# Reordered first loads and a re-timed plan in a fused polysketch attention and ReGLU kernel

## The chip, the cores and the metric

The kernel runs on one core of a Trainium2 chip. The metric is device time in microseconds of one execution, the median over runs. A core has five engines with a queue each: TensorE (PE in the profile, its weight loads PEld), VectorE (DVE), ScalarE (ACT), GpSimd (POOL) and SyncE (SP), which only issues DMAs here. ScalarE can issue DMAs too. Each engine works through its own queue in order and waits on semaphores where data is not there yet. All DMAs run on the same 16 DMA engines.

## The reference

```python
# q, k, v: [4 batches, 4 heads, 1088, 32]; S1, S2: [8, 32]
def phi(x):
    a = einsum('rd,bhsd->bhsr', S1, x)
    b = einsum('rd,bhsd->bhsr', S2, x)
    return einsum('bhsi,bhsj->bhsij', a, b).reshape(..., 64)
q_p, k_p = phi(q), phi(k)
kv  = einsum('bhsf,bhsd->bhfd', k_p, v)
z   = k_p.sum(over s)
num = einsum('bhsf,bhfd->bhsd', q_p, kv)
den = einsum('bhsf,bhf->bhs', q_p, z) + 1e-6
x   = (num / den), heads side by side: [4352 tokens, 128]
out = (relu(x @ w_gate) * (x @ w_val)) @ w_out     # d_ff = 1536
```

Linear attention with a feature map of degree two, then a gated feed-forward layer (FFN) on its output, all in float32 at the borders and mostly in fp16 inside.

## The kernel before

**The stages.** For each batch b the K side (class `K`) loads k, transposes it on VectorE in 32x32 blocks (`kt1`, tile `kT`), sketches it on TensorE (`ksk`), transposes back (`kt2`, tile `kab`), forms the products of the feature map (`kphi`, tile `kp`) on POOL and, for batch 0 in part, on VectorE, casts v to fp16 on ScalarE (`vc`, L599) and multiplies (`kv`, L606). The result is scaled and masked into `bz` on VectorE (`kve`, L613). The Q side (class `Q`, and `G` for a group of 256 or 512 tokens) does likewise with q; the products are `qqp` (L859). They are transposed by TensorE for the first three groups and by a DMA transpose for the other seven (`TURN`; `xpose`, L867), multiplied with `bz` (`num`, L893) and written as x, tile `xT`. The first group is divided by its denominator on VectorE (`x_div`, L900), the others earlier.

**The FFN** (class `F`) is cut into units of at most 512 columns. A unit is: `g` (x with a block of w_gate, L950), relu out of PSUM on ScalarE (L955), `v` (x with w_val, L962), the product on VectorE (L972), and `o` (with w_out, L984). Every sixth unit takes another way: ScalarE copies the `v` result out of PSUM (L967) and POOL multiplies (L977). There are ten groups: 256, 256, 512, then six of 512 and a last of 256 tokens. The weights come as float32 in thirds (`wg0`, `wv0`, `wo0`, ...), into buffers that later hold k, q and v of other batches, and are cast to fp16 by ScalarE or POOL (`CAST`, L425 and L427).

**What sets the order.** The kernel is scheduled by hand: a planner (class `Plan`) gets every step with its engine, an assumed duration (`busy`, `rec`), what it comes after, the PSUM banks that it takes, and a due time. It also gets assumed landing times of the first loads (`LAND`, L404). It plays the steps through, and then they are issued in the order of their planned starts. The planned times do nothing else: on the chip each engine goes through its queue in this order, and waits are for data, buffers and banks alone. `T0` and `U` give a due time to each FFN unit (`T0 + u * U`), from which the others' are worked back.

**The first loads** do not go through the planner. They are issued on SP at the top of the program in this order: k of batch 0 in two pieces, q of batch 0 in two, v of batch 0 in four quarters of 32 partitions (`load_v`, 144 KB each), then the weights' thirds with k of batch 1 among them, and q of batch 1 (L231 to L270). The loads of the later batches are planned steps on SP (`load`, L435), each behind the casts that free its buffer. A DMA takes one of eight semaphores in turn, in order of issue over both issuing engines, and is issued once the DMA that had that semaphore before it has landed.

**Dummies.** `warm(n)` (L326) issues matmuls of a zero tile into a spare PSUM bank, some n columns in all, in pieces of up to 128 columns. The plan's gaps on TensorE before the first FFN matmul are filled with them.

Of the kernel before, what the change touches and what calls it, by code (L numbers as in the profile page):

```python
# [146 lines left out]
def kernel(  # L147
# [87 lines left out]
    nc.sync.dma_start(out=q_sb[0][:, QA:], in_=flat(q, 0)[:, QA:])  # L235
    for a in (0, 2, 1, 3):
        load_v(nc.sync, 0, a)
# [24 lines left out]

    load_w(0)
    load_w(1)
    load_wo(0)
    load_k(nc.sync, 1)
    load_w(2)
    load_wo(1)
    load_wo(2)
    nc.sync.dma_start(out=q_sb[1], in_=flat(q, 1))  # L270

# [54 lines left out]
    def warm(n):  # L326

        while n >= 32:
            m = min(n // 32 * 32, 128)
            nc.tensor.matmul(PS[:, W_BANK, 0:m], zero, zero[:, 0:m], start=True, stop=True)  # L330
            n -= m

# [46 lines left out]
    PE0, WARM = 4.15, 8.0  # L379
    P = Plan({"PE": PE0, "DVE": 3.3, "ACT": 4.2, "POOL": 3.8, "SP": 13.3, "DMA": 0.0}, range(7))  # L380
    P.banks[W_BANK] = 13.0
    P.banks[S_BANK] = 6.0
    l_sx = Lease()
    T0, U, SLACK = 11.0, 0.68, 0.25
    D1 = 0.2
# [12 lines left out]
    def act(cols):  # L398
        return cols / 1200.0 + 0.045

    def pool(cols):
        return cols * 0.00188 + 0.07

    LAND = {"k0a": 3.6, "S": 4.3, "k0b": 4.25, "q0a": 5.6, "q0b": 7.35, "v0": 9.95,  # L404
            "wg0": 10.35, "wv0": 11.0, "wg1": 11.65, "wv1": 12.3, "wo0": 12.95, "k1": 15.6,
            "wg2": 16.25, "wv2": 16.9, "wo1": 17.5, "wo2": 18.1, "q1": 19.5}
    land = {n: P.landed(n, t) for n, t in LAND.items()}
    P.free["DMA"] = LAND["q1"]

    def bank(l, i=0):  # L410
        return PS[:, l.banks[i]]

    ws_op = P.add("ACT", "wS", 0.36, make_wS, [land["S"]], rec=0.13)
    wq_op = P.add("POOL", "wq", 0.25, make_wq, [ws_op])
    sa_op = P.add("DVE", "SA", 0.22, make_SA, [land["S"]], rec=0.07)
    wb_op = P.add("DVE", "WB", 0.15, make_WB, [land["S"]], rec=0.07)

    CAST = {"wg0": "ACT", "wv0": "POOL", "wg1": "ACT", "wv1": "POOL", "wo0": "POOL",
            "wg2": "ACT", "wv2": "ACT", "wo1": "ACT", "wo2": "POOL"}
    wcast = {}  # L420
# [12 lines left out]


    def load(name, fn, after):  # L435
        n = 4 if name[0] == "v" else 1
        i = P.add("SP", f"{name} issue", 0.44 * n, fn, after, rec=1.95 - 0.44 * n)
        land[name] = P.add("DMA", name, 2.7 if n == 4 else 1.4, None, [i], rec=0.15)

    load("v1", lambda: load_vs(1), [wcast["wo2"]])  # L440
    load("k2", lambda: load_k(nc.sync, 2), [wcast["wo0"], wcast["wo1"]])
    load("q2", lambda: load_q(nc.sync, 2), [])
    load("v2", lambda: load_vs(2), [wcast["wg2"], wcast["wv2"], land["v1"]])
    load("k3", lambda: load_k(nc.sync, 3), [wcast["wg0"], wcast["wv0"], land["q2"]])
    load("q3", lambda: load_q(nc.sync, 3), [wcast["wg1"], wcast["wv1"], land["q2"]])
    load("v3", lambda: load_vs(3), [land["v2"]])

    class K:


        def __init__(self, b, prev):
# [14 lines left out]
            for n, l in enumerate(self.las):  # L466
                self.sks.append(P.add(
                    "PE", f"ksk {b} {n}", sk32(KX * 32) + 0.04 if b else (0.62, 0.68)[n],
                    lambda n=n: self.sk(n), t1 + [ws_op], take=[l]))
# [17 lines left out]
            cut = [(0, 2), (2, 4), (4, 6), (6, KX)] if b else [(0, 2), (2, 4), (4, 6), (6, 8), (8, KX)]  # L487
            own = [3, 4] if b == 0 else []
            lb = Lease()
# [141 lines left out]
    class Q:  # L631
# [3 lines left out]
        def __init__(self, b, x0, n, i, ks, qt1, old):  # L635
# [9 lines left out]
            if first:  # L645
                la, lc = Lease(), Lease()
                self.la, self.lc = la, lc
                s1 = [P.add("PE", f"qsk {name} {x}", 0.48, lambda x=x: self.sk_tok(x, x + 2),
                            qt1 + [wb_op], take=[la]) for x in range(0, n, 2)]
                t2 = P.add("ACT", f"qt2 {name}", act(2 * cols), self.t2_tok, s1 + old, drop=[la],  # L650
                           rec=0.13)
                la.left += n
                lt = Lease()
                self.lt = lt
                at = P.add("PE", f"qaT {name}", 0.85, self.aT, qt1 + [sa_op], take=[lt])
                ate = P.add("ACT", f"qaTe {name}", act(256), self.aTe, [at], drop=[lt], rec=0.13)
                s2 = [P.add("PE", f"qc {name}", 0.45, self.cx, [ate, ks[0].zc_op], take=[lc])]
                o1 = P.add("DVE", f"bw {name}", dve(cols) + 0.03, self.mul_ps, s2 + [t2] + old,
                           drop=[lc], rec=0.09)
                e, eng = "DVE", nc.vector  # L660

            else:
                self.l4 = [Lease(2), Lease(2)]
                s1 = P.add("PE", f"qsk {name}", cols / 600.0 + 0.28 + 0.37 * (n > NX),
                           self.sk, qt1 + wcs + [wq_op], take=self.l4)
# [133 lines left out]
    class G:  # L799


        def __init__(self, qs, b, ks, x0, n, i, col, old, how):
# [12 lines left out]
            else:  # L815
                phis.append(P.add("POOL", f"qphi {name}", pool(n * 256),
                                  lambda: self.phi(nc.gpsimd, 0, n), [qs.o4] + old))
            if how == "DMA":
                pt = P.add("SP", f"qtd {name}", 1.28, self.xpose, phis + old, rec=0.7)
                pt = P.add("DMA", f"qtd {name}", 0.6, None, [pt], rec=0.5)  # L820
            else:
# [85 lines left out]
    class F:  # L907


        def __init__(self, u, grp, qg, js, prev, old):  # L910
# [13 lines left out]
                      due=t + 0.35)  # L924
            vv = P.add("PE", f"v {u}", cost, self.v, [qg.x_op, wcast[f"wv{third}"]], take=[lv], due=t + 0.2)
# [117 lines left out]
    for n, (b, x0, w, parts) in enumerate(sets):  # L1043
# [6 lines left out]
        for gb, y, m in parts:  # L1050
# [80 lines left out]
```

## Time and profile before

| what | value |
|---|---|
| median of 3 runs | 101.46 us (101.31 to 104.93) |
| profiled execution | 102.56 us, of which the span of instructions is 100.8 |
| granted TensorE clock | 1.000 |
| PE / PEld busy | 95.1 / 66.4 us |
| DVE / ACT / POOL busy | 83.8 / 82.2 / 59.9 us |
| moved by DMA | 13.28 MB, mean 132 GB/s |
| PE's part in the chain that ended last | 78% |

The span runs from the first instruction to the last; the execution's own time has 1.8 us around it. Busy time of TensorE is the time in which a matmul is under way, and matmuls are pipelined, so a busy TensorE can still be losing time between them. The chain that ended last is followed back from the last instruction, at each step to what released it.

```profile
L330 PE MATMUL ps<-zero 128*128 128x128 f16 (+2 forms) x85 | 7.7, 257 | 1.0 <-DVE maskkv L295 1.0
L593 POOL TENSOR_TENSOR kp<-kab 128x512 f16<-128x512 f32 (+1 forms) x15 | 17.1, 1162 | 5.0 <-DVE kab L549 5.0
L859 POOL TENSOR_TENSOR qqp<-qan,qabc 128x1024 f16<-128x1024 f32 (+1 forms) x9 | 15.7, 1763 | 0.1
```

Three rows of the costliest groups: line, engine, operation, output and inputs with their shapes, count; then busy us, mean ns of one; then the idle time of the engine just before them and what ended it.

### The profile page before, as it was taken

How to read it: one execution, taken by the hardware profiler on the slowest of the kernel's cores; microseconds unless marked ns; L12 is line 12 of the kernel's file. 1: busy time of each engine (PE TensorE's matmuls, PEld its weight loads, DVE VectorE, ACT ScalarE, POOL GpSimd, SP SyncE). 2: the span in 40 equal slices, each digit the busy share in tenths (PEclk: the TensorE clock that was granted, in tenths of full speed). 3: DMA queues.
4: the chain of work that ended last, by engine and by line, in shares of the span. 5: the costliest groups of instructions: out<-in, count | busy, mean ns of one | idle time of the engine just before them, and what ended most of it. 6: DMA issues, size and time to landing. Idle time of an engine off the chain costs nothing.

```text
span 100.8 us, 3139 instructions
## 1 busy us (share of the span) xinstructions
PE 95.1 (94%) x1191; PEld 66.4 (66%) x1191; DVE 83.8 (83%) x181; ACT 82.2 (82%) x162; POOL 59.9 (59%) x64
## 2 busy tenths in 40 slices
PE   6999997999999899999999999999999999999960
PEld 6959895678775466656756676667666666667940
DVE  5989959899999989999998679978768587795960
ACT  3411968997999978999977769899899999989940
POOL 7157269399999399349973993489960314033100
PEclk9999999999999999999999999999999999999999
DMA  2999999499943696300426003001481300120031
GB/s 44 321 272 294 408 403 417 166 309 272 386 131 108 145 136 163 104 7 0 104 52 156 7 0 104 7 7 37 121 182 37 81 24 0 52 59 0 4 100 52
DMA packets 16783, 13.28 MB, mean 132 GB/s; under 512 B 8064, under 2 KB 14464, under 8 KB 16768
## 3 DMA queue, kind: packets, MB, share of 16 engines
q1 hardware_dynamic: 16736, 13.08, 45.8%
q8 instruction: 9, 0.15, 0.6%
q14 instruction: 6, 0.05, 0.1%
q10 hardware_dynamic: 32, 0.00, 0.0%
HBM read 9.14 MB, written 2.23 MB: 113 GB/s over the span
## 4 chain that ended last, share of the span: by engine, by line
PE 78%; POOL 7%; ACT 5%; DMA 3%; issue 2%; DVE 2%; ACTq 0%
PE ps L984 19%; PE ps L950 18%; PE ps L962 17%; PE ps L330 7%; POOL qqp L859 4%; PE ps L893 3%; ACT g_sb L955 3%; PE ps L728 3%; DMA qpt<-qqp 3%; PE ps L536 2%; PE ps L606 2%; POOL kp L593 1%; PE ps L564 1%; PE ps L877 1%; DVE qabc L734 1%
## 5 line engine op out<-in xcount | busy, mean ns | idle before, releaser
L972 DVE TENSOR_TENSOR ht<-g_sb,ps 128x512 f16<-128x512 f16 (+1 forms) x87 | 55.4, 672 | 10.1 <-ACT g_sb L955 5.5
L955 ACT ACTIVATE g_sb<-ps 128x512 f16<-128x512 f32 (+1 forms) x103 | 57.1, 610 | 4.9 <-PE ps L950 4.1
L950 PE MATMUL ps<-xT,wg 128*128 128x512 f16 (+1 forms) x120 | 38.3, 348 | 0.4 <-ACT wg L425 0.4
L984 PEld LDWEIGHTS <-ht 128*128 128x128 f16 x408 | 28.8, 98 | 14.0 <-POOL ht L977 2.5
L984 PE MATMUL ps<-wo,ht 128*128 128x128 f16 x408 | 36.5, 219 | 0.2
L962 PE MATMUL ps<-xT,wv 128*128 128x512 f16 (+1 forms) x120 | 36.5, 348 | 0.0
L977 POOL TENSOR_TENSOR ht<-g_sb,v_sb 128x512 f16<-128x512 f16 x16 | 18.7, 1170 | 19.3 <-ACT v_sb L967 13.2
L593 POOL TENSOR_TENSOR kp<-kab 128x512 f16<-128x512 f32 (+1 forms) x15 | 17.1, 1162 | 5.0 <-DVE kab L549 5.0
L962 PEld LDWEIGHTS <-wv 128*128 128x128 f16 x120 | 13.0, 115 | 5.1 <-issue 1.1
L859 POOL TENSOR_TENSOR qqp<-qan,qabc 128x1024 f16<-128x1024 f32 (+1 forms) x9 | 15.7, 1763 | 0.1
L950 PEld LDWEIGHTS <-wg 128*128 128x128 f16 x120 | 13.1, 114 | 3.7 <-issue 0.9
L967 ACT COPY v_sb<-ps 128x512 f32<-128x512 f32 x16 | 9.7, 605 | 0.0
L330 PE MATMUL ps<-zero 128*128 128x128 f16 (+2 forms) x85 | 7.7, 257 | 1.0 <-DVE maskkv L295 1.0
L330 PEld LDWEIGHTS <-zero 128*128 128x128 f16 x85 | 6.7, 119 | 1.4 <-DVE maskkv L295 1.0
L992 ACT ACTIVATE o_sb<-ps 128x512 f32<-128x512 f32 (+1 forms) x10 | 5.5, 546 | 1.9 <-PE ps L984 1.9
L599 ACT CAST v<-v 128x576 f16<-128x576 f32 x8 | 5.3, 700 | 1.5 <-DMA v<-in_v_dram 1.4
L734 DVE STREAM_TRANSPOSE qabc<-ps 128x512 f32<-128x512 f32 (+2 forms) x8 | 5.4, 695 | 0.7 <-PE ps L728 0.6
L1024 DVE STREAM_TRANSPOSE qT<-q_sb 128x576 f32<-128x576 f32 (+4 forms) x10 | 6.0, 611 | 0.0
L905 ACT CAST xT<-ps 128x512 f16<-128x512 f32 (+1 forms) x9 | 4.9, 550 | 1.1 <-PE ps L893 1.1
L893 PE MATMUL ps<-qpt,bz 128*128 128x512 f16 (+2 forms) x26 | 5.3, 305 | 0.4 <-DMA qpt<-qqp 0.4
L525 DVE STREAM_TRANSPOSE kT<-k_sb 128x544 f32<-128x544 f32 (+2 forms) x8 | 5.6, 725 | 0.0
L606 PEld LDWEIGHTS <-kp 128*128 128x128 f16 (+1 forms) x72 | 3.6, 98 | 1.3 <-issue 0.2
(85 smaller groups left out, 63.9 us busy)
## 6 DMA issues: line engine op xcount, KB each, us to landing
v<-in_v_dram SPq DMA_DIRECT2D x15, 144.0 KB, 4.5
out_dram<-o_sb SPq DMA_DIRECT2D x28, 64.0 KB, 1.7
k_sb<-in_k_dram SPq DMA_DIRECT2D x3, 544.0 KB, 5.4
q_sb<-in_q_dram SPq DMA_DIRECT2D x3, 544.0 KB, 7.1
k_sb<-in_moe_w_out_dram SPq DMA_DIRECT2D x2, 256.0 KB, 5.9
q_sb<-in_q_dram SPq DMA_DIRECT2D x1, 416.0 KB, 5.2
k_sb<-in_k_dram SPq DMA_DIRECT2D x1, 288.0 KB, 2.9
k_sb<-in_k_dram SPq DMA_DIRECT2D x1, 256.0 KB, 3.0
```

Source lines behind the costliest of these rows:

```text
L330: nc.tensor.matmul(PS[:, W_BANK, 0:m], zero, zero[:, 0:m], start=True, stop=True)
L593: eng.tensor_tensor(out=self.kp[:, lo:hi].rearrange("p x g (i a c) -> p (x g i) a c", i=2, a=R), in0=src[:, 0, :, :, None].to_broadcast([1 ...
L734: nc.vector.transpose(self.abc[:, 0:self.n, 2 * i:2 * i + 2].rearrange("p x h f -> p h x f"), PS[:, b0:b1 + 1, 0:self.n * 32].rearrange("p ...
L859: eng.tensor_tensor(out=self.qp[:, lo:hi].rearrange("p x g (i a c) -> p (x g i) a c", i=2, a=R), in0=a_in[:, :, :, None].to_broadcast([128 ...
L893: nc.tensor.matmul(o[:, 0:n * 128].rearrange("f (x t) -> f x t", x=n)[:, :, t], self.ks[b or 0].bz[:, p], self.pt[:, 0:n, p, t], start=(p ...
L950: nc.tensor.matmul(bank(self.lg)[:, y * W:(y + 1) * W], wblock(wg, j), x, start=True, stop=True, skip_group_check=True)
L955: nc.scalar.activation(out=self.gs[:, 0:self.cols], in_=bank(self.lg)[:, 0:self.cols], func=ACTF.Relu)
L962: nc.tensor.matmul(bank(self.lv)[:, y * W:(y + 1) * W], wblock(wv, j), x, start=True, stop=True, skip_group_check=True)
L967: nc.scalar.copy(out=self.vs, in_=bank(self.lv))
L972: nc.vector.tensor_tensor(out=self.ht[:, 0:w], in0=self.gs[:, 0:w], in1=bank(self.lv)[:, 0:w], op=ALU.mult)
L977: nc.gpsimd.tensor_tensor(out=self.ht, in0=self.gs, in1=self.vs, op=ALU.mult)
L984: nc.tensor.matmul(o[:, s], self.ht[:, y * W + s * 128:y * W + (s + 1) * 128], wo[:, j // 4, (j % 4) * DM:(j % 4 + 1) * DM], start=(j == 0 ...
```

## The change

- v of batch 0: quarters 0 and 1 stay on SP, quarters 2 and 3 are issued by ScalarE, behind its step `wS`.
- The weights, k of batch 1 and q of batch 1 become a planned step on SP (`ring`) that the planner sets behind ScalarE's issue. Their order among themselves is as before.
- `warm` makes dummies of up to four times 128 columns in one matmul; from 8.0 us of planned time on, 0.1 us of each gap is left unfilled.
- The casts of `wv2` and `wo1` go from ScalarE to POOL.
- For batch 0, VectorE keeps only the last kp block (`own = [4]`); the fourth goes to POOL.
- The loads of k, q and v of batch 3 are put behind the DMA transpose of the fifth group (`gs[4].turn`); those of k and q no longer wait for q of batch 2.
- `LAND`, `U` and durations of several steps are changed.

```diff
-    for a in (0, 2, 1, 3):
+    for a in (0, 1):
         load_v(nc.sync, 0, a)
...
         while n >= 32:
-            m = min(n // 32 * 32, 128)
-            nc.tensor.matmul(PS[:, W_BANK, 0:m], zero, zero[:, 0:m], start=True, stop=True)
-            n -= m
+            m, w = (min(n // 128, 4), 128) if n >= 128 else (1, n // 32 * 32)
+            nc.tensor.matmul(PS[:, W_BANK, 0:m * w], zero,
+                             zero[:, None, 0:w].to_broadcast([128, m, w]), start=True, stop=True)
+            n -= m * w
...
-    T0, U, SLACK = 11.0, 0.68, 0.25
+    T0, U, SLACK = 11.0, 0.65, 0.25
...
-        return cols / 1200.0 + 0.045
+        return cols / 1200.0 + 0.062
...
-    LAND = {"k0a": 3.6, "S": 4.3, "k0b": 4.25, "q0a": 5.6, "q0b": 7.35, "v0": 9.95,
-            "wg0": 10.35, "wv0": 11.0, "wg1": 11.65, "wv1": 12.3, "wo0": 12.95, "k1": 15.6,
-            "wg2": 16.25, "wv2": 16.9, "wo1": 17.5, "wo2": 18.1, "q1": 19.5}
+    LAND = {"k0a": 3.6, "S": 4.3, "k0b": 4.25, "q0a": 5.3, "q0b": 6.8, "v0": 8.5, "wg0": 9.2,
+            "wv0": 9.84, "wg1": 10.48, "wv1": 11.12, "wo0": 11.76, "k1": 13.12, "wg2": 14.76,
+            "wv2": 15.4, "wo1": 16.04, "wo2": 16.68, "q1": 18.04}
...
+    half_v = P.add("ACT", "v issue", 0.9, lambda: [load_v(nc.scalar, 0, a) for a in (2, 3)], [ws_op],
+                   due=0.0)
+    def load_ring():
+        load_w(0)
+        load_w(1)
+        load_wo(0)
+        load_k(nc.sync, 1)
+        load_w(2)
+        load_wo(1)
+        load_wo(2)
+        nc.sync.dma_start(out=q_sb[1], in_=flat(q, 1))
+    ring = P.add("SP", "ring", 7.7, load_ring, [half_v])
...
-            "wg2": "ACT", "wv2": "ACT", "wo1": "ACT", "wo2": "POOL"}
+            "wg2": "ACT", "wv2": "POOL", "wo1": "POOL", "wo2": "POOL"}
...
-    load("q2", lambda: load_q(nc.sync, 2), [])
+    load("q2", lambda: load_q(nc.sync, 2), [ring])
...
-    load("k3", lambda: load_k(nc.sync, 3), [wcast["wg0"], wcast["wv0"], land["q2"]])
-    load("q3", lambda: load_q(nc.sync, 3), [wcast["wg1"], wcast["wv1"], land["q2"]])
+    load("k3", lambda: load_k(nc.sync, 3), [wcast["wg0"], wcast["wv0"]])
+    load("q3", lambda: load_q(nc.sync, 3), [wcast["wg1"], wcast["wv1"]])
...
-                    "PE", f"ksk {b} {n}", sk32(KX * 32) + 0.04 if b else (0.62, 0.68)[n],
+                    "PE", f"ksk {b} {n}", sk32(KX * 32) + 0.04 if b else (0.47, 0.52)[n],
...
-            own = [3, 4] if b == 0 else []
+            own = [4] if b == 0 else []
...
-                at = P.add("PE", f"qaT {name}", 0.85, self.aT, qt1 + [sa_op], take=[lt])
+                at = P.add("PE", f"qaT {name}", 0.62, self.aT, qt1 + [sa_op], take=[lt])
...
-                h = P.add("POOL", f"hp {u}", 1.18, self.hp, [a, a2, old], due=t + 1.3)
+                h = P.add("POOL", f"hp {u}", 1.13, self.hp, [a, a2, old], rec=0.06,
+                          due=t + 1.3)
...
+    for n in ("k3", "q3", "v3"):
+        issue[n].after.append(gs[4].turn)
+        gs[4].turn.succ.append(issue[n])
...
-                warm(int((o.start - at) * (1200 if o.start < WARM else 2280)))
+                warm(int((o.start - at) * 1200) if o.start < WARM else
+                     int((o.start - at - 0.1) * 2280))
```

More of the change, by code (lines that the diff above doesn't have):

```diff
@@ L261, in load_wo @@
             "(f e) m -> f (e m)", e=4))
[L263 to L270, printed above, removed]
     def load_q(eng, b):
@@ L379 @@
     PE0, WARM = 4.15, 8.0
-    P = Plan({"PE": PE0, "DVE": 3.3, "ACT": 4.2, "POOL": 3.8, "SP": 13.3, "DMA": 0.0}, range(7))
+    P = Plan({"PE": PE0, "DVE": 3.3, "ACT": 4.2, "POOL": 3.8, "SP": 4.0, "DMA": 0.0}, range(7))
     P.banks[W_BANK] = 13.0
@@ L432 @@
                          rec={"ACT": 0.13, "DVE": 0.07, "POOL": 0.0}[e])
+    issue = {}
     def load(name, fn, after):
         n = 4 if name[0] == "v" else 1
-        i = P.add("SP", f"{name} issue", 0.44 * n, fn, after, rec=1.95 - 0.44 * n)
+        issue[name] = i = P.add("SP", f"{name} issue", 0.44 * n, fn, after,
+                                rec=1.95 - 0.44 * n)
         land[name] = P.add("DMA", name, 2.7 if n == 4 else 1.4, None, [i], rec=0.15)
@@ L663, in __init__ @@
                 self.l4 = [Lease(2), Lease(2)]
-                s1 = P.add("PE", f"qsk {name}", cols / 600.0 + 0.28 + 0.37 * (n > NX),
+                s1 = P.add("PE", f"qsk {name}", cols / 600.0 + 0.34 + 0.37 * (n > NX),
                            self.sk, qt1 + wcs + [wq_op], take=self.l4)
@@ L815, in __init__ @@
             else:
-                phis.append(P.add("POOL", f"qphi {name}", pool(n * 256),
+                phis.append(P.add("POOL", f"qphi {name}", pool(n * 256) - 0.02 * n,
                                   lambda: self.phi(nc.gpsimd, 0, n), [qs.o4] + old))
@@ L819, in __init__ @@
                 pt = P.add("SP", f"qtd {name}", 1.28, self.xpose, phis + old, rec=0.7)
+                self.turn = pt
                 pt = P.add("DMA", f"qtd {name}", 0.6, None, [pt], rec=0.5)
@@ L924, in __init__ @@
                       due=t + 0.35)
-            vv = P.add("PE", f"v {u}", cost, self.v, [qg.x_op, wcast[f"wv{third}"]], take=[lv], due=t + 0.2)
+            vv = P.add("PE", f"v {u}", cost, self.v, [qg.x_op, wcast[f"wv{third}"]], take=[lv], rec=0.07,
+                       due=t + 0.2)
             if self.pool:
```

## The prediction

> **What bounds the kernel now.** I read the page's slices first, then the sums by stage, then the timeline of the first 21 us, then the waits of 13 to 21 us and the chain of 20 to 38 us.
>
> ```profile
> PE   6999997999999899999999999999999999999960
> DMA  2999999499943696300426003001481300120031
> ```
>
> TensorE is full from the third of the 40 slices (2.5 us each) to the last but one, so the end is set by when real matmuls begin and by how often they wait. The DMA engines are full for the first 18 us and never again: the start is a loading phase. The sums by stage have, for each engine, busy us and instructions, then clock, DMA share and GB/s:
>
> ```profile
> 6.00:8.00 2.00, 1.98 (x40) 1.29 (x26) 1.95 (x7) 0.38 (x1) 1.59 (x2) 1.00 1.07 240
> 8.00:10.00 2.00, 2.00 (x39) 1.86 (x48) 1.97 (x8) 0.27 (x2) 1.54 (x2) 1.00 1.05 300
> 10.00:12.00 2.00, 2.00 (x64) 1.70 (x65) 1.97 (x8) 2.00 (x5) 0.61 (x1) 1.00 1.06 404
> ```
>
> While v is moved (6 to 8 us) the engines are as full (1.07) as while weights are moved (1.06), but carry 240 GB/s, not 404. VectorE is full from 6 to 12 us (1.95 to 1.97 of 2.00), POOL is not.
>
> ```profile
> 2.63 1.86 SPq L216 DMA_DIRECT2D v<-in_v_dram  x4
> 6.82 0.38 ACT L743 ACTIVATE aT<-ps 128x256 f32<-128x256 f32 x1 [1.93 <-PE ps L739]
> 7.31 0.69 DVE L593 TENSOR_TENSOR kp<-kab,ps 128x512 f16<-128x512 f32 x1
> 9.99 1.25 ACT L599 CAST v<-v 128x576 f16<-128x576 f32 x2 [1.37 <-DMA v<-in_v_dram]
> 10.97 0.61 POOL L427 CAST wv<-k_sb 128x512 f16<-128x512 f32 x1 [1.43 <-DMA k_sb<-in_moe_w_val_dram]
> 11.78 0.29 DVE L613 TENSOR_TENSOR bz<-ps,maskkv 128x128 f16<-128x128 f32 x1
> 13.00 0.36 DVE L900 TENSOR_TENSOR xT<-ps,rdT 128x256 f16<-128x256 f32 x1
> 13.76 0.39 PE L950 MATMUL ps<-xT,wg 128*128 128x256 f16 x2
> 16.02 1.36 DVE L525 STREAM_TRANSPOSE kT<-k_sb 128x544 f32<-128x544 f32 x2
> 19.93 1.17 POOL L977 TENSOR_TENSOR ht<-g_sb,v_sb 128x512 f16<-128x512 f16 x1 [1.50 <-ACT v_sb L967]
> ```
>
> The first FFN matmul (13.76) hangs on x (13.00), that on bz (11.78), that on the cast of v, which began when v had landed (9.99). Before the FFN is fed steadily it waits for casts and copies of ScalarE:
>
> ```profile
> PEld L950 <- ACT wg L425: 0.6, 1, 0.6
> PE ps L877 <- ACT g_sb L955: 0.5, 1, 0.5
> PEld L962 <- ACT wo L425: 0.5, 1, 0.5
> ```
>
> ```profile
> 24.30 0.73 POOL bw L762
> 25.03 1.47 POOL kp L593
> 26.50 0.59 POOL qan L794
> 28.17 3.88 POOL qqp L859 x2
> 32.33 2.79 DMA qpt<-qqp
> 35.17 0.60 PE ps L893 x2
> ```
>
> From 24 to 35 us the chain is off TensorE: POOL, then a DMA transpose, then the x of the fourth group, for which TensorE stood 0.40 us. After 35.77 the chain's rows are TensorE to 94.24. From the starts of the matmuls (0.216 us allowed after one of 512 columns, 0.056 after one of 128) I worked out its lost time: 0.9 us in 15 to 20, 0.7 in 30 to 35, 0.3 and 0.4 in the next two stretches of five, then under 0.3 in each, 0.65 in the tail.
>
> **The change part by part.** The profiled execution took 102.56 us, of which the span is 100.8; the median of the three runs is 101.46. Gains are taken from rows of that span and subtracted from the median, 1.1 us under the profiled run.
>
> *v on two queues.* SP loses two issues (1.86 for four, so 0.93), and its weights start that much sooner, at about 3.6 where 4.53 is shown; the planned order after ScalarE's issue puts no wait on SP, since no data ties them. ScalarE gains two, some 0.9 us behind wS (ends 4.90). It is idle there until 6.82, released by TensorE, so the cost is 0; without that cover 0.9. When does the last of v land? Now at about 9.95. k0, q0 and v are 1,664 KB, and v's 576 KB at 240 GB/s are 2.4 us, at 404 they would be 1.4. Best case 1.0 us sooner. Worst: ScalarE issues at 4.9 and 5.4, SP at 3.6 and 4.1, and two weight blocks (512 KB at 404 GB/s, 1.3 us) get ahead of it: 1.3 later. I take 0.7 sooner, nearest to the 404 row, because weights' packets will lie beside v's. By the Trainium skill, "DMA: Bandwidth & Descriptors", section "Issuing engines are not separate DMA queues", a second issuer saves issue time only, so v would land no sooner; no run so far shows two loaded queues. What follows from a v that lands no sooner is the second rival below.
>
> *kp moved.* `own` gives the fourth kp block of batch 0 to POOL: VectorE loses 0.69 (7.31) and most of the 0.35 transpose ahead of it, some 0.8 us of its full stretch. POOL's three take 3.13 and end at 9.54, a fourth ends at 10.6, inside the 1.43 idle that ends at 10.97: cost 0, uncovered 1.04. But the kv matmuls now wait for 10.6 whatever v does: two halves of 0.26 us issue and their latency put bz at about 11.3, 0.45 ahead of 11.78.
>
> *Dummies.* Same columns, fewer instructions, 0.1 us less at each gap. They now run to 13.8, while x ended at 13.36; bz to its matmul took 0.27 (12.07 to 12.34), so the FFN could go at 13.63: 0.13 to gain. A 512-column dummy under way when work is ready costs up to 0.24 (four of 0.061, as 22 took 1.35). Bounds -0.13 and +0.24, taken at -0.1. The start is 0.55 sooner.
>
> *Casts wv2 and wo1 to POOL.* ScalarE loses about 1.26 us at 17.67 to 18.8, in front of the relu and copy that TensorE waited for. The three waits above sum to 1.6, of which 1.0 to 1.1 lies behind casts. I take 0.7, between 0 and 1.1. POOL gains 1.22 (0.61 each), covered by the 1.50 idle ahead of 19.93; uncovered, 1.22 is added to POOL's chain.
>
> *k3, q3 behind the second DMA transpose.* Their two issues (21.15, 21.63) move past the loads of v2, a store and two transposes on SP, to about 35. k3's first transpose ran at 40.08, q3's at 50.23, with landings of 5.4 and 7.1 us: the second has room, the first is moved along by the plan to its next place, and matmuls use it at 52. Cost 0; if k3 were needed at 40, 0.4. v2 and the store no longer queue behind them: nobody waits for these, so no gain.
>
> *Due dates and durations* (0.65 for 0.68 us, eviction 0.017 longer, product on POOL 1.13 with 0.06) change the order of every queue. No row prices that. After 35 us 1.6 us of lost time is left outside the tail, so between 0.5 lost and 0.8 gained; I take 0.5 gained, as the copy's and product's durations come closer to the rows (0.61 and 1.17).
>
> *Sum.* TensorE's side of the first 35 us gains 0.55 + 0.7 = 1.25. The chain through POOL gains about 0.8 (what loads land sooner by). Where they meet, at 35.17, the gain lies between: 1.05. With 0.5 behind it 1.55, so 101.46 - 1.55 = **99.9 us**. Own range: 0.5 gained, if the cast and order terms come to nothing on balance (101.0), to 0.55 + 1.1 + 0.8 = 2.45, if both come whole (99.0).
>
> **The rivals.**
>
> *VectorE is held by k1 (slower).* The plan is told that k1 lands at 13.12 (15.6 before). It has VectorE idle from 13.63 to 14.82, so kT of batch 1 (1.36 at 16.02) will be queued there, ahead of the products that free PSUM banks. If k1 lands at its old 15.3, VectorE stands 2.2 us past the written time, TensorE fills its banks and stops: 2.2 lost, and with the start's gain not collected 103.7; up to 105 if the plan's later orders fray. For: wv1 was written 12.30 and POOL waited 1.82 until 13.40. Against: k1 follows v in the same full queue and moves with it, and an early kT helps POOL's chain. It decides if k1 lands more than some 1.5 us after VectorE reaches its transpose. Chance 0.22.
>
> *v lands no sooner.* Then bz stays at 11.78 and only dummies and casts are left: 0.1 + 0.7, so 100.7. For: the DMA engines are full either way. Against: 240 GB/s at a share of 1.07 says that v's packets, not the bytes, fill them. Chance 0.07. The rule quoted from the Trainium skill would give this one.
>
> *All gains meet.* POOL's chain starts with k1, and if kT is sooner by more than TensorE's side, the 0.57 us lost at 34.6 goes as well: 1.25 + 0.6 + 0.8 = 2.65, so 98.8. For: POOL had 4.96 us of idle before 20 us (1.43, 1.82, 0.21, 1.50). Against: 2.26 of it is spent on kp and casts. Chance 0.20.
>
> **How the numbers follow.** The forecast has 0.51. 2% of 101.46 is 2.03 us, about what a measurement of this kernel can tell from no change, so faster is under 99.43 and slower over 103.49. Of the forecast 0.16 lies under 99.43, the lower fifth of its range with some weight for casts that give more than I took, and 0.35 within. Faster 0.16 + 0.20 = 0.36; same 0.35 + 0.07 = 0.42; slower 0.22. The range takes the third rival's 98.8 with 0.1 below it and the near edge of the first, 103.7, leaving out some 0.16 of that above and 0.03 below: 98.7 to 103.7.
>
> **What would show it.** v on two queues: the cast of v begins under 9.5, not at 9.99. kp: four POOL blocks in a row, no POOL idle before wv, bz at about 11.3. First FFN matmul at about 13.2. Casts: no TensorE wait for ScalarE's wg or wo around 18. The chain: the fourth group's matmuls at about 34 rather than 35.17. The first rival shows as a VectorE idle ended by the DMA of k1, of which there is none now. I am wrong if POOL, full from 20 to 32, takes 1 us more ahead of its qqp products, or if new TensorE waits appear after 40 us.

## The result, and the profile after

| | before | after |
|---|---|---|
| median | 101.69 us (101.31 to 104.93, 4 runs) | 106.38 us (105.55 to 107.55, 4 runs) |
| profiled execution, its span | 102.56, 100.8 | 107.2, 105.4 |
| mean granted TensorE clock | 1.000 | 0.968 |
| cast of v begins | 9.99 | 13.80 |
| first FFN matmul | 13.76 | 19.67 |
| last matmul ends | 97.70 | 102.33 |

The ratio of after to before is 1.035, 95% interval 1.0273 to 1.0427: slower. Some executions of a kernel, before or after the change, take some per cent longer than its others: all ratios are of the faster ones alone, the medians are of all, and both profiles, before and after, are of slower ones. The first FFN matmul is 5.91 us later and the last matmul 4.63 later, so the whole loss lies ahead of 20 us and 1.28 us is won back behind it. Forecast were 99.9 us and a first FFN matmul at 13.2.

The slices of the page, 2.6 us each:

```profile
PE   6997049999899998999999999999999999999970
PEclk9999965599999999999999999999999999999999
DMA  2999999505827148992042600302346120030031
```

TensorE has a hole in the fifth slice, which was not there before, and the clock is down in the two or three slices behind it. The DMA engines are as full as before until 18 us, but they carry less for a time: 283 GB/s from 10 to 12 us and 319 from 12 to 14, where the kernel before had 404 and 405. By stage (busy us and instructions of PE, PEld, DVE, ACT, POOL, then clock, DMA share, GB/s):

```profile
10.00:12.00 2.00, 0.00 (x1) 0.03 (x1) 2.00 (x7) 0.00 (x0) 1.22 (x2) 1.00 1.08 283
12.00:14.00 2.00, 0.00 (x0) 0.00 (x0) 0.08 (x1) 0.20 (x1) 0.61 (x1) 0.94 1.06 319
14.00:16.00 2.00, 1.47 (x22) 1.47 (x22) 0.00 (x0) 2.00 (x5) 0.61 (x1) 0.50 1.02 388
```

From 10 to 14 us TensorE, and from 12 to 14 nearly everything, stands. When it goes on, its clock is 0.50, from 13.77 to 20.60 in the clock's records. The timeline tells what was waited for:

```profile
3.56 0.43 SPq L256 DMA_DIRECT2D k_sb<-in_moe_w_gate_dram  x1
4.03 0.43 SPq L257 DMA_DIRECT2D k_sb<-in_moe_w_val_dram  x1
4.46 0.39 ACTq L216 DMA_DIRECT2D v<-in_v_dram  x1
7.37 0.34 ACTq L216 DMA_DIRECT2D v<-in_v_dram  x1
7.75 0.38 ACT L754 ACTIVATE aT<-ps 128x256 f32<-128x256 f32 x1 [2.86 <-PE ps L342]
13.80 1.25 ACT L610 CAST v<-v 128x576 f16<-128x576 f32 x2 [4.92 <-DMA k_sb<-in_moe_w_out_dram]
17.42 0.29 DVE L624 TENSOR_TENSOR bz<-ps,maskkv 128x128 f16<-128x128 f32 x1 [5.34 <-PE ps L617]
19.67 0.59 PE L964 MATMUL ps<-xT,wg 128*128 128x256 f16 x2
```

SP has sent off two weight blocks before ScalarE's first load of v (4.46), and by 5.42 two more. ScalarE's second load follows only at 7.37: by the records of the semaphores, the one that it takes in the turn had been that of q's second piece, which landed at 7.35. By the same records `wg0` landed at 9.36, `wv0` at 10.68, v's third quarter at 11.71, `wg1` at 12.01, `wv1` at 12.84, v's last quarter at 13.74 and `wo0` at 14.12. The cast begins 0.06 us behind v's last quarter. The row names the load of `wo0` as its releaser, which is inferred and here wrong, since that landed 0.32 us after the cast had begun; the order of landing is what settles it.

Of the chain of waits, from 37 to 41 us:

```profile
37.47 2.80 DMA qpt<-qqp
40.31 0.59 PE ps L905 x2
```

The matmuls of the fourth group behind their DMA transpose, at 35.17 before and forecast at about 34, are still on the chain, at 40.31: this meeting has moved 5.14 us with the start.

### The profile page after: what moved, and what is told of

Same layout as the page of the kernel before. It is cut to its first block, busy times and chain, and to the rows that moved or that the text cites. A ratio compares the mean times of both kernels' runs of the same rounds, so it can differ in the third digit from the quotient of the medians.

```text
span 105.4 us, 3027 instructions
## 1 busy us (share of the span) xinstructions
PE 95.9 (91%) x1128; PEld 63.4 (60%) x1128; DVE 83.2 (79%) x180; ACT 80.8 (77%) x160; POOL 62.0 (59%) x67
## 4 chain that ended last, share of the span: by engine, by line
PE 72%; DMA 13%; POOL 5%; DVE 2%; ACT 2%; SPq 2%; issue 1%; ACTq 0%; POOLq 0%
PE ps L998 19%; PE ps L964 19%; PE ps L976 18%; DMA k_sb<-in_moe_w_out_dram 5%; DMA v<-in_v_dram 5%; PE ps L905 4%; POOL qqp L871 4%; DMA qpt<-qqp 3%; PE ps L739 2%; PE ps L322 2%; PE ps L617 2%; POOL ht L991 1%; PE ps L547 1%; DVE qT L1038 1%; PE ps L889 1%
## 5 line engine op out<-in xcount | busy, mean ns | idle before, releaser
L964 PE MATMUL ps<-xT,wg 128*128 128x512 f16 (+1 forms) x120 | 39.3, 351 | 0.0
L976 PE MATMUL ps<-xT,wv 128*128 128x512 f16 (+1 forms) x120 | 39.1, 350 | 0.0
L998 PE MATMUL ps<-wo,ht 128*128 128x128 f16 x408 | 37.0, 219 | 0.2 <-DVE ht L986 0.2
L604 POOL TENSOR_TENSOR kp<-kab 128x512 f16<-128x512 f32 (+1 forms) x16 | 18.1, 1153 | 3.7 <-DVE kab L560 3.7
L964 PEld LDWEIGHTS <-wg 128*128 128x128 f16 x120 | 13.2, 115 | 3.6 <-issue 1.5
L617 PE MATMUL ps<-v,kp 128*128 128x64 f16 (+1 forms) x72 | 4.7, 205 | 4.5 <-ACT v L610 4.5
L322 PE MATMUL ps<-zero 128*128 128x512 f16 (+4 forms) x22 | 7.8, 486 | 1.0 <-DVE maskkv L287 1.0
```

What stands on the lines that cost most here:

```text
L322: nc.tensor.matmul(PS[:, W_BANK, 0:m * w], zero, zero[:, None, 0:w].to_broadcast([128, m, w]), start=True, stop=True)
L604: eng.tensor_tensor(out=self.kp[:, lo:hi].rearrange("p x g (i a c) -> p (x g i) a c", i=2, a=R), in0=src[:, 0, :, :, None].to_broadcast([1 ...
L617: nc.tensor.matmul(m[:, 64 * p:64 * p + 64], self.kp[rows, x, p], v16[self.b][rows, 2 * p:2 * p + 2, x * D:(x + 1) * D], start=(x == 0 and ...
L964: nc.tensor.matmul(bank(self.lg)[:, y * W:(y + 1) * W], wblock(wg, j), x, start=True, stop=True, skip_group_check=True)
L976: nc.tensor.matmul(bank(self.lv)[:, y * W:(y + 1) * W], wblock(wv, j), x, start=True, stop=True, skip_group_check=True)
L998: nc.tensor.matmul(o[:, s], self.ht[:, y * W + s * 128:y * W + (s + 1) * 128], wo[:, j // 4, (j % 4) * DM:(j % 4 + 1) * DM], start=(j == 0 ...
```

## The experiments

The leading theory, theory A where the expectations use letters, was that loads are served in order of issue over both issuing engines, so that what SP issues ahead of ScalarE's loads lands ahead of them, and that the late v is the loss. Against it stood that the loss is elsewhere in the change (kp, casts, dummies, order). The times of the kernel before went from 101.69 to 102.74 between batches, so ratios are given, each with its 95% interval against runs on the same chip.

**The rest of the change without the two queues** (e1). All four quarters of v go out on SP again, ahead of the weights; ScalarE's planned step does nothing.

```diff
-    for a in (0, 1):
+    for a in (0, 2, 1, 3):
         load_v(nc.sync, 0, a)
...
-    half_v = P.add("ACT", "v issue", 0.9, lambda: [load_v(nc.scalar, 0, a) for a in (2, 3)], [ws_op],
+    half_v = P.add("ACT", "v issue", 0.9, lambda: None, [ws_op],
                    due=0.0)
```

> The changed kernel, but all four quarters of the first v are issued by SP ahead of the weights, as before the change; the planned step on ScalarE stays and does nothing, so the plan and every queue's order are the same. Theory A (loads are served in order of issue over both issuing engines, so ScalarE's quarters stand behind the weights that SP has issued by then, and that is the whole loss): v's cast begins at 9.9 to 10.1 us, the first FFN matmul at 13.0 to 13.8, the time is 100 to 101.7. Rival B (the re-timed plan, with its casts and kp on POOL and its early landing times, costs time by itself): v's cast begins as early, but the time stays above 103. Rival C (any load from ScalarE's queue is slow, whatever is ahead of it) also gives 100 to 101.7 and is told apart by the run with the hold.

Measured: 102.06 us, ratio 0.9972 (0.9933 to 1.0012); cast of v at 10.33. All three numbers of the expectation (cast, first FFN matmul, time) were missed, the time by 0.36 us, but the loss is gone with the two queues, so it is not in the rest of the change. This profiled execution had its clock at 0.50 from 11.10 to 14.51, and its first FFN matmul at 15.49, yet its last matmul ended at 97.73, as before.

**The two queues alone** (e2). The kernel before, with only the third and fourth quarter moved to ScalarE behind `wS`.

```diff
-    for a in (0, 2, 1, 3):
+    for a in (0, 1):
         load_v(nc.sync, 0, a)
...
     ws_op = P.add("ACT", "wS", 0.36, make_wS, [land["S"]], rec=0.13)
+    half_v = P.add("ACT", "v issue", 0.9, lambda: [load_v(nc.scalar, 0, a) for a in (2, 3)], [ws_op],
+                   due=0.0)
```

> The kernel before, with one part of the change alone: quarters 2 and 3 of the first v are issued by ScalarE behind wS, the weights stay where they were on SP, and the plan's landing times, casts, kp and dummies are those of before. Theory A: the quarters land behind the weights issued ahead of them, v's cast begins at 11.5 to 14 us instead of 9.99, the first FFN matmul 2 to 5 us later than 13.76, and the time is 103.5 to 106. Rival B (the re-timed plan costs the time): 101 to 102, like before. If the loads of two queues shared the engines evenly, v's cast would begin at 9.5 to 10 and the time be 101 to 102 too.

Measured: 108.19 us, ratio 1.057 (1.0462 to 1.0678). ScalarE issued at 4.47 and 7.20, the cast began at 13.80 and the first FFN matmul at 19.15. This one edit costs more alone than the whole change does. The mechanism came out as expected, the time above the 103.5 to 106 of the expectation.

**SP held until ScalarE has issued** (e5). Behind its two loads ScalarE writes one element of the first weight buffer, so that SP's first weight load has data to wait for.

```diff
-    half_v = P.add("ACT", "v issue", 0.9, lambda: [load_v(nc.scalar, 0, a) for a in (2, 3)], [ws_op],
+    def issue_v():
+        for a in (2, 3):
+            load_v(nc.scalar, 0, a)
+        nc.scalar.copy(out=wst[0][0][0:1, 0:1], in_=zero[0:1, 0:1])
+
+    half_v = P.add("ACT", "v issue", 0.9, issue_v, [ws_op],
                    due=0.0)
```

> The changed kernel, with the weights really held back: behind its two v issues ScalarE writes one element of the buffer into which the first weight block is loaded, so SP's first weight issue waits for ScalarE. Theory A: v's two late quarters are now ahead of all weights, v's cast begins at 9.0 to 10.2 us and the time is 99.5 to 102; the weights are issued from about 5.5 on. Rival C (ScalarE's queue is slow by itself, some 4 us from issue to first packet): the cast begins after 11 us and the time stays above 103. Rival B: the cast begins early and the time stays above 103.

Measured: 102.54 us, half a microsecond above what was expected, ratio 0.997 (0.9911 to 1.003). From its timeline:

```profile
4.85 0.44 ACTq L216 DMA_DIRECT2D v<-in_v_dram  x1
5.55 0.35 SPq L256 DMA_DIRECT2D k_sb<-in_moe_w_gate_dram  x1
9.95 1.24 ACT L615 CAST v<-v 128x576 f16<-128x576 f32 x2 [1.67 <-DMA v<-in_v_dram]
```

ScalarE's second load goes out at 4.85: with no weight load ahead of it, it gets another semaphore in the turn. v lands as in the kernel before (cast 9.95 against 9.99), on two queues, so two queues by themselves do not make the loss. No gain shows either: landings differ from one execution to the next, and the cast began at 9.09 to 10.36 in the seven traces that have v on SP ahead of the weights, and at 9.95, 10.41, 10.60 and 11.36 in the four that have the hold (e5 and, further down, e15, e7 and e10). `aT` is at 6.79 again. What holds the loads up is seen in the sums by queue. These are of the changed kernel, first from 4.5 to 8.5 us, then from 8.5 to 12.7 (q1 is SP's queue, q10 ScalarE's; packets, MB, share of 16 engines):

```profile
q1 hardware_dynamic: 574, 0.96, 101.1%
```

```profile
q1 hardware_dynamic: 497, 0.91, 79.6%
q10 hardware_dynamic: 288, 0.30, 28.5%
```

ScalarE's first load was issued at 4.46, and in the four microseconds after it not one packet of its queue ran, while SP's earlier loads did. Then its packets ran from 8.56 to 12.65, beside those of SP's queue: the first ran before `wg0`, issued ahead of them, had landed (9.36). So it is the landings that follow the order of issue; the packets of neighbours in that order overlap. In e5 its packets ran from 5.86 to 8.91. The Trainium skill, "DMA: Bandwidth & Descriptors", section "Queues, rings and completion order", says that each DMA engine goes in turn through the queues that have work, packet by packet; a load on a queue of its own would then get a share at once. In these runs it did not at first, and did from 8.56 on. Whether its packets were not yet made, or waited in their queue, no run here shows.

**How much goes ahead** (e13). The same hold, but in the third weight block's buffer, so that two blocks (512 KB) are issued ahead of ScalarE's loads, and those go out at 4.47 and 4.85. The hold is the only difference from e5.

```diff
-        nc.scalar.copy(out=wst[0][0][0:1, 0:1], in_=zero[0:1, 0:1])
+        nc.scalar.copy(out=wst[0][1][0:1, 0:1], in_=zero[0:1, 0:1])
```

> The held kernel, but ScalarE's write now stands in the buffer of the third weight block: two blocks (512 KB) are issued ahead of ScalarE's v, the rest behind it. Theory A (order of issue): the cast of v begins 1.3 us later than with everything held (512 KB at 404 GB/s), at 11.0 to 11.5 us against 9.95 held and 13.80 in the changed kernel, and the time lies between theirs, 102.5 to 104. If what is ahead in the queue doesn't matter, the cast begins at 10 and the time is 101 to 102.5.

Measured: 104.92 us, ratio 1.0208 (1.0057 to 1.0358). The cast is at 12.74, not 11.0 to 11.5: right in direction, but the two blocks cost 2.79 us against e5, where the bytes at 404 GB/s gave 1.3, and the time is above the 102.5 to 104 expected. ScalarE's packets ran from 7.89 to 11.94, beside SP's. From 10 to 12 us, with both queues at work, the DMA engines were as full as ever (a share of 1.05) but carried 227 GB/s, less than with v (240) or with weights (404) in the kernel before. The other 1.06 us, to 13.80, go with the issue that was held until 7.37 and the blocks that passed it in that time. So the order of issue explains that v is late, but its price per block is twice what was put on it; the lower rate is part of that, and why the rate falls is not settled.

**v issued by ScalarE ahead of everything** (e6). The two loads stand behind the first activation, and were issued at 1.75 and 2.13, ahead of the first two quarters on SP.

```diff
     nc.scalar.activation(out=scr, in_=zero[0:1, 0:1], func=ACTF.Relu)
+    for a in (2, 3):
+        load_v(nc.scalar, 0, a)
...
-    half_v = P.add("ACT", "v issue", 0.9, lambda: [load_v(nc.scalar, 0, a) for a in (2, 3)], [ws_op],
+    half_v = P.add("ACT", "v issue", 0.9, lambda: None, [ws_op],
                    due=0.0)
```

> The changed kernel, but ScalarE issues its two quarters of v right behind its first activation, at about 3.2 and 3.7 us, not behind wS; nothing holds the weights, which SP issues from about 3.6 on. Theory A (service in order of issue over both queues): one weight block at most stands ahead of the second quarter, so v's cast begins at 9.7 to 10.6 us and the time is 101 to 103, against 13.80 and 105.6 of the changed kernel. Rival C (ScalarE's queue is slow by itself, some 4 us to the first packet): first packet after 7 us, cast after 11, time above 103.

Measured: 104.01 us, ratio 1.0172 (1.0108 to 1.0235), above the 101 to 103 expected. ScalarE's packets ran from 3.42 to 6.80 and v was cast at 9.94. The order of issue holds here too, but for one pair: ScalarE's first load landed at 5.88, ahead of q's first piece (6.26), which SP had issued 0.07 us before it. And now q lands late, its first piece at 6.26 and its second at 8.21 (4.90 and 7.35 in the changed kernel). TensorE waited 0.62 us behind the first and 0.42 behind the second, the clock went to 0.50 from 9.11 to 15.94, and the first FFN matmul came at 16.50. Whatever goes first, something else goes later: the DMA engines are full.

**The clock** (e4). The change with 9,216 more columns of dummies ahead of the first `kv` matmuls, so that TensorE is busy while v is late.

```diff
             m = bank(self.lm)
+            if self.b == 0 and lo == 0 and 0 in pp:
+                warm(9216)
             for x in range(lo, hi):
```

> The changed kernel with 9,216 more columns of dummy matmuls (3.8 us at full clock) ahead of the first kv matmul, where TensorE stood idle from 10.0 to 14.5 us. Everything else is the same. If the granted clock fell to 0.5 from 13.6 to 20.5 us because TensorE stood idle, it now stays at 1.0, the stretch from the first kv matmul to the first FFN matmul shrinks from 5.1 us to about the 3.1 us of before, and the time falls by 1.5 to 2.0 us, to about 104. If the clock has nothing to do with it, the time stays at 105.5 to 106.5.

Measured: 104.33 us, ratio 1.0201 (1.0128 to 1.0275), the clock 1.00 in all of it, the cast at 13.72, `bz` at 16.10 and the first FFN matmul at 17.57 (17.42 and 19.67 in the changed kernel), as expected. Of the 3.5% some 1.5 are the clock (the two intervals just touch), and what is left goes with the late v.

How long TensorE must stand for this, the traces do not settle. In the changed kernel the clock fell to 0.50 after 3.8 us of standing, and stayed there for 6.83 us. In e1 it fell at 11.10, after two short waits:

```profile
8.74 0.41 PE L589 MATMUL ps<-zs,L 128*128 128x32 f32 x2 [0.42 <-DVE zs L583]
11.05 0.46 PE L617 MATMUL ps<-v,kp 128*128 128x64 f16 x6 [0.71 <-ACT v L610]
```

e6, too, had only its waits of 0.62 and 0.42 us ahead of its drop. In e5 a wait of 0.79 us brought none. The time at 0.50 was 3.4 us in e1, e2 and e13 and 6.83 in e6. The Trainium skill, "TensorE: Matmul & The Clock Gate", section "The HAM clock gate", has the clock halve after a window of about 3.4 us without work and gives it back after a window of work. The changed kernel fits that; e1 and e6 do not, since TensorE had work in most of the 3.4 us before the drop.

**The other parts, one by one on the kernel before.** Casts of `wv2` and `wo1` on POOL (e9), the fourth kp block on POOL (e11), dummies of up to 512 columns (e12).

```diff
-            "wg2": "ACT", "wv2": "ACT", "wo1": "ACT", "wo2": "POOL"}
+            "wg2": "ACT", "wv2": "POOL", "wo1": "POOL", "wo2": "POOL"}
```

> The kernel before with one part of the change alone: the casts of wv2 and wo1 on POOL, not ScalarE. The predicted term was 0.7 us (bounds 0 and 1.1): 100.4 to 101.5. If POOL has no room for them where they fall (1.22 us on the way to the fourth group's products), it is 101.5 to 102.7.

```diff
-            own = [3, 4] if b == 0 else []
+            own = [4] if b == 0 else []
```

> The kernel before with one part alone: own = [4], the fourth kp block of batch 0 on POOL. My step said: VectorE 0.8 us freer, no price on POOL, nothing gained while v lands at 9.95. So 101 to 102.3. If POOL's order is the bound, up to 1.0 us slower.

```diff
-            m = min(n // 32 * 32, 128)
-            nc.tensor.matmul(PS[:, W_BANK, 0:m], zero, zero[:, 0:m], start=True, stop=True)
-            n -= m
+            m, w = (min(n // 128, 4), 128) if n >= 128 else (1, n // 32 * 32)
+            nc.tensor.matmul(PS[:, W_BANK, 0:m * w], zero,
+                             zero[:, None, 0:w].to_broadcast([128, m, w]), start=True, stop=True)
+            n -= m * w
```

> The kernel before with one part alone: dummies of up to 512 columns, the same columns in all. Clock theory by columns: a busy TensorE is a busy TensorE, so no change, 101.3 to 102.4 and a granted clock of 1.0 through the first 20 us. If fewer, longer dummies hold the clock worse, the clock shows 0.5 in a stretch before 20 us and the time rises by 1 to 2 us.

Measured: casts 1.0034 (0.9997 to 1.0072), kp 1.001 (0.9962 to 1.0057), dummies 1.0292 (1.019 to 1.0393). The first two are worth nothing that can be told from 1. The third was a surprise. Its first FFN matmul came at 13.87, as before, and its clock stayed at 1.00; up to 70 us it kept pace. Then, from its timeline, SP and TensorE, and the sums by queue from 69.8 to 71.0 us:

```profile
68.99 3.44 SPq L1002 DMA_DIRECT2D out_dram<-o_sb  x4
72.97 4.02 SPq L868 DMA_TRANSPOSE qpt<-qqp  x3
...
76.41 0.59 PE L894 MATMUL ps<-qpt,bz 128*128 128x512 f16 x2 [2.33 <-DMA qpt<-qqp]
```

```profile
q1 hardware_dynamic: 270, 0.12, 38.9%
q8 instruction: 1, 0.02, 8.8%
```

and the same two rows of SP before:

```profile
69.08 1.77 SPq L1001 DMA_DIRECT2D out_dram<-o_sb  x4
71.39 3.90 SPq L867 DMA_TRANSPOSE qpt<-qqp  x3
```

Four stores that took 1.77 us to issue take 3.44, since one of them takes 2.13 (at 69.83) instead of 0.43. The transposes behind it on SP go out 1.58 late and TensorE stands 2.33. While that store was being issued, one packet of 16,384 bytes ran on q8, the queue of the instructions. Such packets come some ten microseconds apart and take 0.9 to 1.7 us. In the kernel before, all three of SP's issues of loads and stores over 0.7 us meet one (10.94 with 10.79, 26.61 with 26.60, 35.05 with 34.68), and in e12 all six. Not every meeting is long: e12's block at 50.74 fell on issues of 0.31 and 0.63 us.

**Moving the blocks** (e14). With 26 matmuls in place of 85, e12's blocks come later than those of before. e14 is e12 with its first three stretches of dummies in 128-column pieces again, which is 39 matmuls and as many weight loads more; its other dummies keep up to 512 columns.

```diff
+    short = 0
     def warm(n):
+        nonlocal short
+        short += n >= 32
...
-            m, w = (min(n // 128, 4), 128) if n >= 128 else (1, n // 32 * 32)
+            m, w = (min(n // 128, 4 if short > 3 else 1), 128) if n >= 128 else (1, n // 32 * 32)
```

> The kernel before with dummies of up to 512 columns as in e12, but the first three stretches (28, 8 and 16 dummies) in 128-column pieces as before: 78 more TensorE instructions than e12 in the first 10 us, nothing else changed. Theory (a block of TensorE's instructions is loaded while SP issues the store at 69.8, and the transpose queued behind it comes late): the blocks load about 3 us sooner, the store's issue is back at 0.43 us, TensorE does not stand at 73.7, and the time is that of the kernel before, 101.8 to 102.8, ratio 0.995 to 1.005. If another issue is met instead, the loss shows at that issue. Rival (dummies of 512 columns cost by themselves): the time stays at 104 or more, ratio 1.02 and over, with the idle at the same place.

Measured: 102.64 us, ratio 0.9934 (0.9878 to 0.9989). The block of 69.90 comes at 65.08, the four stores take 1.77 us again and TensorE does not stand. The rival, that long dummies hurt by themselves, falls. Three issues still meet a block (10.04, 36.19, 78.96) and cost little; that nothing urgent is behind them on SP would explain it, and was not tested. That a meeting can make the issue long is shown by these pairs; what the two share is not. That the blocks are TensorE's is inferred: 78 instructions more on TensorE moved this one by 4.82 us. The Trainium skill, "Runtime: NRT & Kernel Launch", section "Instruction fetch mechanics", has blocks of 16 KiB (256 instructions), fetched ahead by the sequencer at a cost that is mostly hidden. For SP's issue it was not hidden here: 2.13 us instead of 0.43.

**Towards a better version.** e7 is e5 with `LAND` set to the landings seen in e5 (`v0` 9.9, `wg0` 10.3, `k1` 15.1 and so on); e8 is e1 with the `LAND` of the kernel before; e10 is e7 with 1,536 columns of dummies ahead of the first `kv`; e15 is e7 with dummies of 128 columns.

```diff
-    LAND = {"k0a": 3.6, "S": 4.3, "k0b": 4.25, "q0a": 5.3, "q0b": 6.8, "v0": 8.5, "wg0": 9.2,
-            "wv0": 9.84, "wg1": 10.48, "wv1": 11.12, "wo0": 11.76, "k1": 13.12, "wg2": 14.76,
-            "wv2": 15.4, "wo1": 16.04, "wo2": 16.68, "q1": 18.04}
+    LAND = {"k0a": 3.6, "S": 4.3, "k0b": 4.25, "q0a": 5.3, "q0b": 7.35, "v0": 9.9, "wg0": 10.3,
+            "wv0": 10.9, "wg1": 11.55, "wv1": 12.15, "wo0": 12.8, "k1": 15.1, "wg2": 15.3,
+            "wv2": 16.2, "wo1": 16.6, "wo2": 17.4, "q1": 18.7}
```

> The kernel with the weights held behind ScalarE's v, and its table of landing times replaced by what that run's trace showed: q0b 7.35, v0 9.9, wg0 10.3, wv0 10.9, wg1 11.55, wv1 12.15, wo0 12.8, k1 15.1, wg2 15.3, wv2 16.2, wo1 16.6, wo2 17.4, q1 18.7. Only the planner reads it, so only orders change. Theory D (the early table puts steps in front of data that has not landed: kv on TensorE from 9.9 to 10.7, kT of batch 1 on VectorE for 1.1 us): these waits go, x of the first group is ready at 13.0 to 13.4 rather than 13.76, and the time falls by 0.5 to 1.5 us to 99.5 to 101. Rival E (what waits there costs nothing, because POOL's and the DMAs' order is what counts): within 0.5 us of the held kernel.

> The changed kernel with all four quarters of v on SP ahead of the weights and the landing table of before: what is left of the change is casts and kp on POOL, dummies, due dates, durations and the place of batch 3's loads. My predicted terms for these, without the loads, were 0.1 for dummies, 0.7 for casts and 0.5 for due dates: 1.3 us, so 100 to 100.5 if the terms were right. If the table matters (theory D), it is faster than the run with v on SP and the changed table by 0.5 us or more; if not (rival E), the two are within 0.5 us.

> The held kernel with the true landing table, and 1,536 more dummy columns (0.64 us at full clock) ahead of the first kv matmul, so that TensorE does not stand while v is cast. If the spread of that kernel's runs (100.66 to 105.71 us) comes from a clock that falls in some executions for want of work before 11 us, the median comes nearer its fastest, 100.5 to 101.2. If not, 101.3 to 101.7 as it was, or 0.3 more where the dummies delay the kv matmuls.

> e7 (the change with the weights held behind ScalarE's loads of v, and the plan told the landings as seen) with its dummies in 128-column pieces as in the kernel before. Theory (the form of the dummies is worth nothing by itself): same as e7, 101.0 to 101.9, ratio about 0.99. Rival (the long dummies cost something of their own, or leave the clock lower): 100.0 to 100.9, ratio 0.98 or under.

| | median us | ratio | 95% interval |
|---|---|---|---|
| e7, SP held, true landings | 101.46 | 0.9909 | 0.9859 to 0.9958 |
| e15, as e7, short dummies | 101.53 | 0.9918 | 0.9874 to 0.9962 |
| e10, as e7, guard of the clock | 102.01 | 0.9954 | 0.9906 to 1.0002 |
| e8, v on SP, landings of before | 102.39 | 1.0024 | 0.9988 to 1.006 |

e7 and e15 are the best of all kernels, 0.9% under the kernel before, and alike: no worth of the dummies' form by itself shows. e7 stayed above the 99.5 to 101 of theory D, and e8 missed its expectation. So did e10: its clock was down from 11.19 to 14.60 in the profiled execution, before the guard's columns ran (12.55). TensorE had stood 1.01 us from 8.03 on for `zs` of VectorE, which had waited 1.1 us for q; q's second piece landed at 8.31 there, at 7.63 in e7. The guard stands behind that wait. e5 and e7 overlap in their intervals, so that `LAND` alone gives the 0.9% is not shown.

## Why the prediction was wrong

**The step that failed: "When does the last of v land?"** It took 0.7 us sooner, with 1.0 sooner and 1.3 later as bounds. Measured: 3.81 later by the cast. The mechanism of the worst bound was the right one, two weight blocks that get ahead, and it was set aside for a row that says how dense the packets are, not who is served first. By that row the loads were taken to run side by side from the start, at the rate of the 404 row "because weights' packets will lie beside v's". In the changed kernel v's third quarter got no packet for 4.1 us after its issue, and when the packets did lie side by side the engines carried 283 GB/s (10 to 12 us). And the bound was itself too small three times over: two blocks cost 2.79 us (e13) and not 1.3, ScalarE's second issue was held until 7.37 and more blocks passed it (1.06), and TensorE, which stood for 4.5 us, went on at half its clock (some 1.5% of the time by e4). No part of the prediction had a price for the clock. The 0.8 us that POOL's chain was to gain from sooner loads went the same way: k of batch 1 landed at 16.77, not at 15.32.

**"The planned order puts no wait on SP, since no data ties them"** was right, and was the undoing. The change means the weights to go behind ScalarE's issues, and nothing makes them. The sentence was used to credit SP's weights with 0.93 us sooner; it should have been used to ask what they would now be ahead of. With the tie put in (e5), the loss is gone.

**"ScalarE's two issues cost 0"**, covered by its idle time up to 6.82: the cover held for issues of 0.93 us. It did not hold for an issue that waits for a semaphore. Which semaphore the second issue would take in the turn was not worked out, though the rule of the turn was known; `aT` came 0.93 late. In e5, where the turn falls otherwise, it costs nothing.

**kp.** POOL's four blocks took 4.15 us and ended at 10.61, against 10.6 forecast, and cost nothing, as forecast. But `bz` at 11.3 was not to be had: in e11, with v landing as before, it is at 11.89. It waits for the cast of v, which kp does not move.

**Dummies, -0.1**: e15 against e7 shows no difference, e14 gives 0.7% (0.1 to 1.2) less, but e12 2.9% more. The step counted columns and gaps. That fewer instructions also move the blocks in which they are loaded was not thought of, and is nothing that a sum of durations could have held.

**Casts, 0.7**: nothing of it came; e9 gives 0.34% (-0.03 to 0.72) more, not 0.7% less. The waits were real, but the moved casts did not make them. The wait of 0.6 us was for `wg2`, which stays on ScalarE and is cast ahead of the two that moved: in e9 it is still `PEld L950 <- ACT wg L425: 0.6, 1, 0.6`. The wait for a cast on ScalarE behind it became one for a cast on POOL, `PEld L962 <- POOL wo L427: 0.5, 1, 0.5`.

**k3 and q3, due dates and durations, 0.5**: no run separates them. The change without its loss lies between 0.2% more (e8) and 0.9% less (e7), and e1, e5 and e8 cannot be told from nothing. So at most about 0.9 us is left of all the terms that the sum put at 1.55 together with what v was to give.

**The rivals.** VectorE held by k1, at 103.7, named the right sign and the wrong cause: in the changed kernel VectorE never waits for k1. The wait is seen where v lands in time, in e5:

```profile
DVE kT L541 <- DMA k_sb<-in_k_dram: 1.1, 1, 1.1
```

It is there 1.1 us long, half of the 2.2 forecast, and that kernel is no slower than before. "v lands no sooner", given 0.07, is what two queues do when nothing is issued between (e5). The rule quoted with it, that a second issuer saves issue time only, agrees: cast at 9.95 on two queues, at 9.99 on one. Its argument, that the engines are full either way, was right. The slower time came from a case that was only a bound of a cost and was never made a rival with a time of its own.

## What to carry to other kernels

On the full DMA engines of this kernel a load landed, but for one pair in e6, by its place in the order of issue over both issuing engines. Moving a load to another queue moves it in that order, so write down who issues what and when, with the semaphores that they take in turn, before counting bytes. An order that only a planner knows is no order; tie it with data if it matters. A delay that leaves TensorE without work can be paid twice, the second time at half the clock (1.00 against 0.50 between e4 and the changed kernel); waits of 0.42 and 0.71 us came ahead of such a drop in e1.

## What the hardware showed unexpectedly

- ScalarE's queue got no packet in the 4 us after an issue at 4.46, while loads that SP had issued before it ran on the same engines; from 8.56 us on the packets of both queues ran side by side.
- With packets of v and of weights from both queues side by side, full DMA engines carried less than with either on one queue: 227 GB/s at a share of 1.05 in e13 (10 to 12 us), against 240 at 1.07 and 404 at 1.06 in the kernel before. In the changed kernel it was 283, between the two.
- A 16,384-byte block of instructions, loaded while SP issues a load or a store, can make that issue take 0.7 to 2.3 us instead of 0.33 to 0.43 (e12: 2.13, then 2.33 us of TensorE; e1: 2.29). So the number of TensorE's instructions in the first 10 us decided which store was hit 60 us later (e12 against e14).
- The clock fell to 0.50 where TensorE had stood at most 0.71 us at a stretch in e1, 0.62 in e6 and 1.01 in e10, and did not fall after 0.79 in e5. So kernels that differ little differ in it: e7's profiled execution had 1.00 from 6.5 to 98.6 us, e10's 0.50 from 11.19 to 14.60.
